# A gated linear attention feeding an MLP on one Trainium2 core: two token blocks worked one after the other, and a new hand-written order

## The chip, the cores and the metric

The kernel runs on one core of a Trainium2 chip. The core has five engines that run their own instruction streams: TensorE (PE in the profile: matrix products, with PEld for the loading of weights), VectorE (DVE), ScalarE (ACT), GpSimd (POOL) and the queue engine SyncE (SP), which here issues nearly all DMAs. They wait for one another through semaphores. The metric is device time in microseconds (us). The kernel before took 552.0 us, the median of three runs (550.45 to 552.59).

## The reference

First a gated linear attention for 4 batches, 8 heads, 768 time steps and head size 48, in float32:

```python
for t in range(S):
    state = alpha[:, :, t, :, None] * state + np.einsum('bhd,bhe->bhde', k[:, :, t], v[:, :, t])
    y[:, :, t] = np.einsum('bhd,bhde->bhe', q[:, :, t], state)
```

Its output, as 3072 tokens of 384 features, goes through a gated MLP with 1536 hidden features:

```python
g = x @ w_gate
silu = g * (1.0 / (1.0 + np.exp(-g)))
val = x @ w_val
return (silu * val @ w_out).astype(np.float32)
```

The three weight matrices come as 64-bit numbers. The kernel has to make 32-bit ones of them itself.

## The kernel before

**Attention.** The 768 steps of a batch are cut into four units of 192 steps, 16 units in all. For a unit u the kernel loads alpha, k and q (words La, Lk, Lq of the order) and v (V), turns them so that features lie on partitions, and runs two scans over alpha on DVE (G, the backward one, L429; f, the forward one, L436). k is multiplied with the one (mk), q with the other (q). Then come chunks of 64 steps: K (k turned back), S (scores), a mask (ma), the chunk states (ad, de), Y (outputs), and the split of Y into a high and a low part (yh on ACT, yl on DVE). The first four units (NPE = 4) are turned by TensorE (Ta, Tk, Tq, L378) from a buffer called wide that is filled by p words. Later units are turned by DVE (tr, tk, tq, L355, and kr for K, L498). In before the first four units also use their own forms of scores (L523), of the carry of the state (Bw, L599) and of the outputs (L693 to L710). Later units do scores and carry in one group (L551, L559) and outputs in another (L680), and add the chunk states on DVE where the early form copies them on ACT.

**MLP.** Tokens are worked in seven blocks (BLOCKS), the first two of 384 tokens, which are units 0 and 1, and 2 and 3. A step is one block and one slice f of 128 hidden features: g (gate product), v (value product), sl (SiLU on ACT), h (product on DVE), hh and hl (high and low part), o (output product). Each of g, v and o is nine matmuls of 384 or 512 columns, since every factor is split into a high and a low part and three of the four products are taken.

**Weights.** The 36 pieces of 128 x 384 weights are loaded and cut to 32 bits in 20 groups, w0 to w19: wl loads, v0, v1 and v2 are three integer steps that cut the 64-bit numbers down (L70 to L88), a makes the high part (L291) and p the low part (L295). After w2 a group holds two pieces. w16 is the gate and value slice 10, w17 the output slice 9 and the gate slice 11, w18 the value slice 11 and the output slice 10. A raw group lies in the place that the finished group behind it will have; that of w18 lies where wide is.

**Order.** The text ORDER lists every piece of work as engine:word (t TensorE, v DVE, s ACT, g POOL, y SP), and each engine takes its words strictly in that order. A digit behind @ names a PSUM bank. In before, HSEG = 7: blocks 0 and 1 first take slices 0 to 6 (steps 0 to 6 and 7 to 13), then 7 to 11 (steps 14 to 18 and 19 to 23). Between the halves the partial output sums go to DRAM (ot, os), are loaded back (pl) and added.

Of the kernel before, what the change touches and what calls it, by code (L numbers as in the profile page):

```python
# [8 lines left out]
F32 = mybir.dt.float32  # L9
# [18 lines left out]
NPE = 4  # L28

WIDE = [(u + x, i) for u in range(0, NPE, 2) for x, i in ((0, 0), (1, 0), (0, 2), (0, 1), (1, 1), (1, 2))]  # L30
# [4 lines left out]
FRAME = 2.0 ** 33  # L35
# [60 lines left out]
def main_path(ctx, tc, q, k, v, alpha, w_gate, w_val, w_out, out, flag, spill):  # L96
# [117 lines left out]
    HSEG = 7


    wsp = {}

    wlist = [("g", 0), ("v", 0)]
    for f in range(1, NF):  # L220
        wlist += [("g", f), ("v", f), ("o", f - 1)]
    wlist.append(("o", NF - 1))
    wgroups = [wlist[i : i + 1] for i in range(WSINGLE)] + [wlist[i : i + 2] for i in range(WSINGLE, len(wlist), 2)]

    def weight_dma(dst, kind, f):
        w = {"g": w_gate, "v": w_val, "o": w_out}[kind]
# [107 lines left out]
    state = {}

    def load_t(src, u, i):
        b, t0 = units[u]
        if u < NPE:

            L = Lt_early[i] if i < len(Lt_early) else Lt_early[4 + (i - 4) % 4]  # L340
            rows_load(L, src, u, halves=i == 0)
            return L
        L = Lt[(i + NPE // 2) % NL]
        Lv = L.rearrange("r (g x) -> r g x", g=G)
        if i < 3 * NPE + NL:
# [14 lines left out]
    def widened(u, i, L, eng):  # L360

        Wd = state[u]["wide", i] = Wide[:, WIDE.index((u, i)) % NP]
        n = 2 if u == i == 0 else 1
        for x in range(n):
            js = slice(x * J // n, (x + 1) * J // n)
            (eng.copy if eng is nc.scalar else eng.tensor_copy)(
                out=Wd[:, js, :, 0:D], in_=L.rearrange("p (e j c) -> p j e c", e=2, j=J)[:, js]
            )

    def pe_transposed(u, i, banks):  # L370

        Wd = state[u].pop(("wide", i))
        r = []
        for hf in range(2):
            js = slice(hf * J // 2, (hf + 1) * J // 2)
            pt = ps.tile([P, J // 2, P], F32, tag=banks[hf], name=f"pt{u}_{i}_{hf}")
            for j in range(js.start, js.stop):
                nc.tensor.transpose(pt[:, j - js.start, :], Wd.rearrange("p j e c -> p (j e c)")[:, j * P : (j + 1) * P], ident)  # L378
            r.append((js, pt.rearrange("p j (t g) -> p g t j", g=G)))
        return r  # L380
# [82 lines left out]
    def values_copied(u, eng):  # L463

        Vd = state[u]["V"]
        g0 = 0 if u >= NPE else GF
        for j, r in ((0, slice(BO, P)), (1, slice(0, BO))):
            (eng.copy if eng is nc.scalar else eng.tensor_copy)(
                out=U[j * BO : j * BO + C, :, g0 * D : G * D].rearrange("p c (g e) -> p c g e", e=D),
                in_=Vd[r, :, g0:, VC[j]],  # L470
            )
# [55 lines left out]
    def scores_carry(u, banks):  # L527

        st = state[u]
        KTt, X, Ks, Vd = st["Gs"], st["X"], st["K"], st["V"]  # L530
        st["S"] = [ps.tile([P, 512], F32, tag=banks[f], name=f"s{f}_{u}") for f in range(2)]
        st["sps"] = [t_[:, 0 : GF * T].rearrange("p (g t) -> p g t", g=GF) for t_ in st["S"]]
        A2 = ps.tile([P, 512], F32, tag=banks[2], name=f"A2_{u}")
        cps = [A2[:, x * G * D : (x + 1) * G * D].rearrange("p (g e) -> p g e", e=D) for x in range(2)]
        rest = A2[:, 2 * G * D : (2 * G + GF) * D].rearrange("p (g e) -> p g e", e=D)
        st["whole"] = False
        st["cps"] = [[(slice(0, G), cps[0])], [(slice(0, G), cps[1])], [(slice(GF, G), rest)]]
        if not last_of_batch(u):

            if u > NPE:  # L540
                beside = state[u - 1]["beside"]
            else:
                beside = ps.tile([P, GF * D], F32, tag=banks[3], name=f"A3_{u}").rearrange("p (g e) -> p g e", e=D)
            st["cps"][2].append((slice(0, GF), beside))
        for c in range(NU):
            cs = slice(1 + c * C, 1 + (c + 1) * C)
            cx = slice(c * C, (c + 1) * C)
            for g in range(G):
                for j in range(2):
                    r = slice(j * BO, j * BO + D)  # L550
# [12 lines left out]
    def carry(u, bank, whole=False):

        st = state[u]
        Ks, Vd = st["K"], st["V"]
        st["whole"] = whole
        A2 = ps.tile([P, 512], F32, tag=bank, name=f"A2_{u}")


        at = [512 - (c + 1) * G * D for c in range(NU)]
        cps = [A2[:, a : a + G * D].rearrange("p (g e) -> p g e", e=D) for a in at[:2]]
        last = A2[:, at[2] + GF * D : at[1]].rearrange("p (g e) -> p g e", e=D)
        beside = st["S"][0][:, GF * T : GF * (T + D)].rearrange("p (g e) -> p g e", g=GF)
        st["cps10"] = A2[:, at[1] :].rearrange("p (c g e) -> p c g e", c=2, g=G)
# [38 lines left out]
    def causal(u, i):  # L614

        X, sps = state[u]["X"], state[u]["sps"]
        r, z, f = (
            (slice(0, P), 1, 0) if u >= NPE else (slice(BO, P), 0, 0), (slice(0, BO), 1, 0), (slice(0, P), 1, 1)
        )[i]
        n = r.stop - r.start  # L620
        nc.vector.tensor_tensor(  # L621
            out=X[r, z, f * GF : (f + 1) * GF, :].rearrange("r g (c t) -> r g c t", c=NU),
            in0=sps[f][r].rearrange("r g (c t) -> r g c t", c=NU),
            in1=mask[r].unsqueeze(1).unsqueeze(1).to_broadcast([n, GF, NU, C]), op=ALU.mult,
        )
# [20 lines left out]
    def decay(u, eng):  # L646

        for j in range(2):
            r = slice(j * BO, j * BO + D)
            eng.scalar_tensor_tensor(  # L650
                out=state[u]["V"][r, 0, :, VC[j]], in0=SE[r], scalar=1.0 / FRAME,
                in1=state[u]["Gs"][r, :, 0:1].to_broadcast([D, G, D]), op0=ALU.mult, op1=ALU.mult,
            )
# [606 lines left out]
```

## Time and profile before

| | |
|---|---|
| median of three runs | 552.0 us (550.45 to 552.59) |
| span of the profiled execution | 549.9 us |
| TensorE busy | 531.2 us |
| DVE busy | 387.7 us |
| ACT busy | 264.1 us |
| POOL busy | 129.6 us |
| DMA | 77.66 MB, 141 GB/s on average |

Busy times are sums over the whole span. What a change is worth has to be read from the stretch in which it lies: which engine is waited for there, and how much idle time the others have.

### The profile page before, as it was taken

How to read it: one execution, taken by the hardware profiler on the slowest of the kernel's cores; microseconds unless marked ns; L12 is line 12 of the kernel's file. 1: busy time of each engine (PE TensorE's matmuls, PEld its weight loads, DVE VectorE, ACT ScalarE, POOL GpSimd, SP SyncE). 2: the span in 40 equal slices, each digit the busy share in tenths (PEclk: the TensorE clock that was granted, in tenths of full speed). 3: DMA queues.
4: the chain of work that ended last, by engine and by line, in shares of the span. 5: the costliest groups of instructions: out<-in, count | busy, mean ns of one | idle time of the engine just before them, and what ended most of it. 6: DMA issues, size and time to landing. Idle time of an engine off the chain costs nothing.

```text
span 549.9 us, 13452 instructions
## 1 busy us (share of the span) xinstructions
PE 531.2 (97%) x5365; PEld 477.5 (87%) x5365; DVE 387.7 (71%) x619; ACT 264.1 (48%) x568; POOL 129.6 (24%) x139
## 2 busy tenths in 40 slices
PE   5879999999999999999999999999999999999995
PEld 3769999999999999998888888888888888899994
DVE  6989899998898997987789856476968353212122
ACT  5778754245334335423423513343335475447691
POOL 5454344142440122110202321012100030011011
PEclk9989999999999999999999999999999999999999
DMA  8889557574455656535464543546246434355321
GB/s 228 245 232 261 159 149 230 132 217 139 125 147 148 162 141 169 174 97 127 139 162 118 129 125 67 135 116 157 54 113 152 99 99 110 95 155 126 103 65 49
DMA packets 115111, 77.66 MB, mean 141 GB/s; under 512 B 53728, under 2 KB 111968, under 8 KB 115040
## 3 DMA queue, kind: packets, MB, share of 16 engines
q1 hardware_dynamic: 114192, 75.98, 51.9%
q8 instruction: 44, 0.72, 0.6%
q10 hardware_dynamic: 848, 0.74, 0.4%
q14 instruction: 27, 0.22, 0.2%
HBM read 62.52 MB, written 5.90 MB: 124 GB/s over the span
## 4 chain that ended last, share of the span: by engine, by line
PE 94%; DVE 2%; ACT 1%; DMA 1%; POOL 0%; issue 0%; DVEq 0%; POOLq 0%; ACTq 0%
PE g L791 27%; PE v L791 27%; PE ops L847 14%; PE ops L842 14%; PE y L680 3%; PE s L551 2%; PE A L599 1%; PE A L559 1%; PE pt L378 1%; PE kps L482 1%; DVE Gs L429 1%; DMA Le<-in_alpha_dram 1%; PE s L523 0%; ACT AT L927 0%; DVE t L78 0%; PE y L710 0%
## 5 line engine op out<-in xcount | busy, mean ns | idle before, releaser
L791 PE MATMUL g<-xT,w 128*128 128x384 f32 (+1 forms) x756 | 163.4, 360 | 0.0
L791 PE MATMUL v<-xT,w 128*128 128x384 f32 (+1 forms) x756 | 162.8, 359 | 0.0
L791 PEld LDWEIGHTS v<-xT,w 128*128 128x128 f32 x756 | 136.1, 188 | 13.2
L791 PEld LDWEIGHTS g<-xT,w 128*128 128x128 f32 x756 | 135.9, 188 | 13.2
L803 DVE TENSOR_TENSOR h<-h,v 128x384 f32<-128x384 f32 (+1 forms) x84 | 51.2, 609 | 110.6 <-PE v L791 94.3
L814 POOL TENSOR_TENSOR hl<-h,hh 128x384 fp32r<-128x384 f32 (+1 forms) x44 | 50.4, 1146 | 267.0 <-ACT hh L808 250.1
L799 ACT ACTIVATE h<-g 128x384 f32<-128x384 f32 (+1 forms) x84 | 45.0, 536 | 137.7 <-PE g L791 119.7
L808 ACT CAST hh<-h 128x384 fp32r<-128x384 f32 (+1 forms) x84 | 46.6, 555 | 77.6 <-PE ops L842 35.3
L847 PE MATMUL ops<-w,hh 128*128 128x384 f32 x286 | 79.6, 337 | 0.0
L842 PE MATMUL ops<-hh,w 128*128 128x512 f32 x216 | 72.2, 393 | 0.0
L498 DVE STREAM_TRANSPOSE K<-Gs 32x384 f32<-32x384 f32 x96 | 54.7, 570 | 2.0
L847 PEld LDWEIGHTS ops<-w,hh 128*128 128x128 f32 x286 | 52.2, 188 | 0.4
L842 PEld LDWEIGHTS ops<-hh,w 128*128 128x128 f32 x216 | 40.5, 188 | 8.9
L847 PE MATMUL ops<-w,hl 128*128 128x384 f32 x143 | 47.8, 335 | 0.0
L842 PE MATMUL ops<-hl,w 128*128 128x512 f32 x108 | 42.2, 391 | 0.0
L295 POOL TENSOR_TENSOR w<-t,w 128x768 fp32r<-128x768 f32 (+1 forms) x16 | 30.5, 1907 | 34.5 <-ACT w L291 30.8
L814 DVE TENSOR_TENSOR hl<-h,hh 128x384 fp32r<-128x384 f32 (+1 forms) x40 | 26.8, 670 | 8.9 <-ACT hh L808 8.6
L429 DVE TENSOR_TENSOR_SCAN Gs<-AT,Z 128x776 f32<-128x776 f32 x16 | 28.3, 1770 | 4.2 <-ACT AT L927 4.1
L436 DVE TENSOR_TENSOR_SCAN AT<-AT,Z 128x774 f32<-128x774 f32 x16 | 29.9, 1868 | 0.6
L261 ACT ACTIVATE wc<-wc 128x384 f32<-128x384 f32 x36 | 19.9, 553 | 15.6 <-DMA wc<-in_moe_w_gate_dram 8.1
L847 PEld LDWEIGHTS ops<-w,hl 128*128 128x128 f32 x143 | 26.9, 188 | 0.0
L621 DVE TENSOR_TENSOR X<-s,mask 128x384 f32<-128x384 f32 (+1 forms) x36 | 19.3, 552 | 8.6 <-PE s L551 8.1
(140 smaller groups left out, 695.2 us busy)
## 6 DMA issues: line engine op xcount, KB each, us to landing
xT<-X SPq DMA_DIRECT2D x72, 72.0 KB, 2.2
raw<-in_moe_w_gate_dram SPq DMA_DIRECT2D x12, 384.0 KB, 5.0
raw<-in_moe_w_val_dram SPq DMA_DIRECT2D x12, 384.0 KB, 6.2
V<-in_v_dram SPq DMA_DIRECT2D x96, 48.0 KB, 3.3
raw<-in_moe_w_out_dram SPq DMA_DIRECT2D x12, 384.0 KB, 4.7
wc<-in_moe_w_gate_dram SPq DMA_DIRECT2D x12, 384.0 KB, 3.7
wc<-in_moe_w_out_dram SPq DMA_DIRECT2D x12, 384.0 KB, 3.6
wc<-in_moe_w_val_dram SPq DMA_DIRECT2D x12, 384.0 KB, 4.2
```

The source lines that it names most:

```text
L261: nc.scalar.activation(dev, dev, AF.Abs, accum_out=wviol[:, 1, i : i + 1])
L295: eng.tensor_tensor(out=lo, in0=src, in1=hi.bitcast(F32), op=ALU.subtract)
L429: nc.vector.tensor_tensor_scan(Gf[:, ::-1], Af[:, ::-1], Z[:, : 0 : -1], 0.0, op0=ALU.mult, op1=ALU.add)
L436: nc.vector.tensor_tensor_scan(Af, Af, Z[:, 1 : n + 1], Z[:, 0:1], op0=ALU.mult, op1=ALU.add)
L498: nc.vector.transpose(out=bass.AP(k0.tensor, k0.offset, [k0.ap[0], (G * 2 * D, NU), (2 * D, G), (1, 32)]), in_=Kg[j * BO + x : j * BO + x ...
L791: nc.tensor.matmul(pt, wsp[kind, f][a][:, kt * P : (kt + 1) * P], xT[blk][:, b_, kt, :], start=(n == 0), stop=(n == 3 * KT - 1),)
L799: nc.scalar.activation(h, acc.pop(("g", blk, f)), AF.Silu)
L803: nc.vector.tensor_tensor(out=h, in0=h, in1=acc.pop(("v", blk, f)), op=ALU.mult)
L808: nc.scalar.copy(out=hh, in_=acc["h", blk, f])
L814: eng.tensor_tensor(out=hl, in0=acc.pop(("h", blk, f)), in1=hh.bitcast(F32), op=ALU.subtract)
L842: nc.tensor.matmul(ops[blk][i], wsp["o", f][a][:, i * P : (i + 1) * P], h[b_], start=(first and n == 0), stop=(last and n == 2),)
L847: nc.tensor.matmul(ops[blk][i], h[b_][:, i * P : (i + 1) * P], wsp["o", f][a], start=(first and n == 0), stop=(last and n == 2),)
```

## The change

The change does four things. HSEG becomes 12, so that block 0 takes all 12 slices in steps 0 to 11 and block 1 in steps 12 to 23; the partial sums never go to DRAM. A new constant NST = 2 says which units use the early forms of scores, carry, outputs and copies: only units 0 and 1. Units 2 and 3 are still turned by TensorE, but are otherwise worked like later units. The buffers of wide are taken by when they were last read and not by a table, and the carry of the early units may use a bank of its own. ORDER is new up to about step 37; from there on it is the same on all engines.

```diff
-WIDE = [(u + x, i) for u in range(0, NPE, 2) for x, i in ((0, 0), (1, 0), (0, 2), (0, 1), (1, 1), (1, 2))]
+NST = 2
...
-g:im g:is y:La0 g:ik s:pa0 y:La1 t:Ta0@51 y:Lq0 g:iv y:wl2 s:ea0 s:pq0 t:Tq0@52 v:G0 ...
+g:ik y:La0 g:is g:iv y:wl0 s:pa0 v:w0v0 y:Lk0 v:w0v1 y:Lq0 t:Ta0@42 y:La1 v:w0v2 ...
...
-    HSEG = 7
+    HSEG = 12
...
+    wide_read = list(range(-NP, 0))
...
-        L = Lt[(i + NPE // 2) % NL]
+        L = Lt[i % NL]
...
-        Wd = state[u]["wide", i] = Wide[:, WIDE.index((u, i)) % NP]
+        w = min((x for x in range(NP) if wide_read[x] is not None), key=lambda x: wide_read[x])
+        wide_read[w] = None
+        Wd, state[u]["wide", i] = Wide[:, w], w
...
-        g0 = 0 if u >= NPE else GF
+        g0 = 0 if u >= NST else GF
...
-            if u > NPE:
+            if u > NST:
                 beside = state[u - 1]["beside"]
...
-    def carry(u, bank, whole=False):
+    def carry(u, bank, bank2, whole=False):
...
-        beside = st["S"][0][:, GF * T : GF * (T + D)].rearrange("p (g e) -> p g e", g=GF)
+        beside = None
+        if bank2 is not None:
+            beside = ps.tile([P, GF * D], F32, tag=bank2, name=f"A3_{u}").rearrange("p (g e) -> p g e", g=GF)
...
-        if u < NPE:
+        if u < NST:
             todo[f"qc{u}"] = lambda eng: q_odd(u, eng)
...
-            if i < 3 and (i != 1 or u < NPE):
+            if i < 3 and (i != 1 or u < NST):
                 todo[f"ma{u}.{i}"] = lambda eng, i=i: causal(u, i)
...
-        todo[f"S{u}"] = lambda eng, *banks: (scores if u < NPE else scores_carry)(u, banks)
-        if u < NPE:
-            todo[f"Bw{u}"] = lambda eng, bank: carry(u, bank, True)
-        todo[f"Y{u}"] = lambda eng, *banks: (outputs if u < NPE else outputs_quarters)(u, banks)
+        todo[f"S{u}"] = lambda eng, *banks: (scores if u < NST else scores_carry)(u, banks)
+        if u < NST:
+            todo[f"Bw{u}"] = lambda eng, bank, bank2=None: carry(u, bank, bank2, True)
+        todo[f"Y{u}"] = lambda eng, *banks: (outputs if u < NST else outputs_quarters)(u, banks)
```

What this does to the order of instructions is shown at three places. The first is the start of DVE's stream. Gs0 and Gs1 are the results of the backward scans of units 0 and 1, X0 is the product with q, t0 and t2 are weight groups 0 and 2 being cut. Before:

```order
L160 MEMSET Z_87 128x4
L429 SCALAR_TENSOR_TENSOR Gs0_158<-AT_94,Z_87 128x776
L433 RECIPROCAL Z_87<-Gs0_158 128x4
L436 SCALAR_TENSOR_TENSOR AT_94<-AT_94,Z_87 128x774
L453 TENSOR_TENSOR X0_104<-pt0_2_0_150,AT_94 112x128x3
L453 TENSOR_TENSOR X0_104<-pt0_2_1_154,AT_94 112x128x3
L78 SCALAR_TENSOR_TENSOR t2_163<-raw2_145,t2_163 128x384
L429 SCALAR_TENSOR_TENSOR Gs1_201<-AT_94,Z_87 128x776
```

The same place on DVE after the change:

```order
L159 MEMSET Z_87 128x4
L71 TENSOR_SCALAR t0_134<-raw0_130 128x384
L81 SCALAR_TENSOR_TENSOR t0_134<-raw0_130,t0_134 128x384
L87 SCALAR_TENSOR_TENSOR t0_134<-raw0_130,t0_134 128x384
L432 SCALAR_TENSOR_TENSOR Gs0_169<-AT_94,Z_87 128x776
L436 RECIPROCAL Z_87<-Gs0_169 128x4
L439 SCALAR_TENSOR_TENSOR AT_94<-AT_94,Z_87 128x774
L456 TENSOR_TENSOR X0_104<-pt0_2_0_161,AT_94 112x128x3
```

All three cutting steps of weight group 0 have moved ahead of the first scan.

The second place is DVE about the twelfth step of the MLP. h1_3 and h1_4 are hidden products of block 1, h0_8 and h0_9 of block 0 (the second number is the slice), t13 to t18 are weight groups being cut, w16 a finished one. Before:

```order
L78 SCALAR_TENSOR_TENSOR t13_1391<-raw13_1163,t13_1391 128x768
L440 MEMSET AT_94 128x3x2
L803 TENSOR_TENSOR h1_3_1448<-h1_3_1448,v1_3_1433 128x384
L88 SCALAR_TENSOR_TENSOR t14_1371<-raw14_1271,t14_1371 128x768
L814 TENSOR_TENSOR hl1_2_1468<-h1_2_1417,hh1_2_1466 128x384
L88 SCALAR_TENSOR_TENSOR t13_1391<-raw13_1163,t13_1391 128x768
L355 STREAM_TRANSPOSE AT_94<-L1_85 128x4x6x32
L498 STREAM_TRANSPOSE K0_106<-Gs4_1199 32x12x32 x2
L803 TENSOR_TENSOR h1_4_1500<-h1_4_1500,v1_4_1513 128x384
```

About as far along DVE's stream after the change:

```order
L810 TENSOR_TENSOR h0_8_1338<-h0_8_1338,v0_8_1307 128x384
L87 SCALAR_TENSOR_TENSOR t16_1336<-raw16_1090,t16_1336 128x768
L77 SCALAR_TENSOR_TENSOR t17_1365<-raw17_1259,t17_1365 128x768
L821 TENSOR_TENSOR hl0_7_1439<-h0_7_1276,hh0_7_1340 128x384
L77 SCALAR_TENSOR_TENSOR t18_1348<-raw18_703,t18_1348 128x768
L294 TENSOR_TENSOR w16_1437<-t16_1336,w16_1437 128x768
L87 SCALAR_TENSOR_TENSOR t17_1365<-raw17_1259,t17_1365 128x768
L810 TENSOR_TENSOR h0_9_1450<-h0_9_1450,v0_9_1427 128x384
```

At this depth before was cutting groups 13 to 15; now the groups 16 to 18 are there, and slice 8 or 9 of block 0 beside them.

The third place is SP's queue, with the semaphores that each DMA waits for (those called DMAHW only keep the places in the DMA rings apart). raw9 and raw18 are the loads of weight groups 9 and 18, L0 and L1 the rows of unit 4, V1 values of unit 3. Before:

```order
L398 DMA V1_90<-in_v_dram 64x4x48 [waits DMAHW6_49,PE_49,Pool_49]
L398 DMA V1_90<-in_v_dram 64x4x48 [waits DMAHW7_49,PE_49,Pool_49]
L233 DMA raw9_721<-in_moe_w_val_dram 128x3x256 [waits DMAHW0_49]
L230 DMA raw9_721<-in_moe_w_out_dram 128x768 [waits DMAHW1_49]
L398 DMA V1_90<-in_v_dram 64x4x48 [waits DMAHW2_49]
L398 DMA V1_90<-in_v_dram 64x4x48 [waits DMAHW3_49]
L398 DMA V1_90<-in_v_dram 64x4x48 [waits DMAHW4_49]
L398 DMA V1_90<-in_v_dram 64x4x48 [waits DMAHW5_49]
L349 DMA L1_85<-in_k_dram 32x4x288 [waits DMAHW6_49,Pool_49]
```

SP's queue after the change:

```order
L401 DMA V0_89<-in_v_dram 64x4x48 [waits DMAHW6_49]
L401 DMA V0_89<-in_v_dram 64x4x48 [waits DMAHW7_49]
L232 DMA raw18_703<-in_moe_w_val_dram 128x3x256 [waits PE_49,DMAHW0_49,Activation_49,Pool_49]
L229 DMA raw18_703<-in_moe_w_out_dram 128x768 [waits DMAHW1_49]
L349 DMA L0_84<-in_alpha_dram 32x4x288 [waits DMAHW2_49,Pool_49]
L349 DMA L0_84<-in_alpha_dram 32x4x288 [waits DMAHW3_49]
L351 DMA L0_84<-in_alpha_dram 32x4x256 [waits DMAHW4_49]
L351 DMA L0_84<-in_alpha_dram 32x4x256 [waits DMAHW5_49]
L232 DMA raw9_750<-in_moe_w_val_dram 128x3x256 [waits DMAHW6_49]
L229 DMA raw9_750<-in_moe_w_out_dram 128x768 [waits DMAHW7_49]
```

The load of group 18 has moved far forward, ahead of group 9 and of unit 4's rows. It waits for TensorE: the value that it waits for is reached with the last transpose of unit 3's q (Tq3), the last reader of wide, which TensorE has in its stream behind g0, v0, g1 and the scores of unit 2.

## Rows read from the trace of the kernel before

**Rows 1.** The page: header, and busy time of each engine

```profile
span 549.9 us, 13452 instructions
PE 531.2 (97%) x5365; PEld 477.5 (87%) x5365; DVE 387.7 (71%) x619; ACT 264.1 (48%) x568; POOL 129.6 (24%) x139
```

**Rows 2.** Stretches: length, busy PE, PEld, DVE, ACT, POOL; PEclk, DMA share, GB/s

```profile
6.80:40.00 33.20, 26.56 (x450) 22.52 (x451) 30.71 (x41) 23.93 (x57) 14.31 (x21) 0.95 0.89 246
40.00:107.20 67.20, 66.95 (x684) 64.93 (x683) 62.08 (x85) 40.13 (x81) 26.29 (x22) 1.00 0.67 189
28.00:42.00 14.00, 10.60 (x241) 9.17 (x240) 12.15 (x20) 10.29 (x26) 7.86 (x9) 0.88 0.83 237
42.00:56.00 14.00, 14.00 (x233) 13.34 (x222) 13.55 (x21) 11.89 (x29) 5.69 (x5) 1.00 0.98 262
```

**Rows 3.** Timeline of TensorE: start, duration, engine, line, operation, count

```profile
45.42 1.81 PE L791 MATMUL g<-xT,w 128*128 128x384 f32 x9
...
49.11 0.93 PE L523 MATMUL s<-X,Gs 48*64 48x64 f32 x48
...
50.47 0.38 PE L599 MATMUL A<-V,K 128*48 128x96 f32 x4
...
52.69 0.57 PE L482 MATMUL kps<-ident,Gs 112*64 112x112 f32 x4
...
103.27 1.72 PE L791 MATMUL g<-xT,w 128*128 128x384 f32 x9
104.83 1.72 PE L791 MATMUL v<-xT,w 128*128 128x384 f32 x9
...
111.17 0.27 PE L551 MATMUL s<-X,Gs 48*64 48x64 f32 x2
...
112.71 0.45 PE L847 MATMUL ops<-w,hh 128*128 128x384 f32 x1
```

**Rows 4.** Timeline of DVE, the idle time before in brackets

```profile
6.82 1.77 DVE L429 TENSOR_TENSOR_SCAN Gs<-AT,Z 128x776 f32<-128x776 f32 x1 [3.80 <-ACT AT L927]
...
11.72 0.55 DVE L78 SCALAR_TENSOR_TENSOR t<-raw,t 128x384 uint32<-128x384 uint32 x1
...
17.81 2.48 DVE L78 SCALAR_TENSOR_TENSOR t<-raw,t 128x384 uint32<-128x384 uint32 x2
...
38.99 1.02 DVE L728 TENSOR_TENSOR Y<-y,Y 112x384 fp32r<-112x384 f32 x2 [1.71 <-ACT Y L724]
...
106.67 0.55 DVE L803 TENSOR_TENSOR h<-h,v 128x384 f32<-128x384 f32 x1
```

**Rows 5.** DVE by line and shape: count, busy us, mean ns, idle before

```profile
L498 DVE STREAM_TRANSPOSE K<-Gs 32x384 f32<-32x384 f32 x96 | 54.7, 570 | 2.0
L436 DVE TENSOR_TENSOR_SCAN AT<-AT,Z 128x774 f32<-128x774 f32 x16 | 29.9, 1868 | 0.6
...
L803 DVE TENSOR_TENSOR h<-h,v 128x384 f32<-128x384 f32 x48 | 26.5, 552 | 50.4 <-PE v L791 39.8 <-ACT ac L422 4.0 <-ACT ac L423 3.7
...
L355 DVE STREAM_TRANSPOSE AT<-L 128x768 f32<-128x768 f32 x12 | 19.6, 1631 | 0.1
...
L88 DVE SCALAR_TENSOR_TENSOR t<-raw,t 128x768 uint32<-128x768 uint32 x16 | 15.2, 952 | 0.2
...
L644 DVE TENSOR_TENSOR V<-A,V 48x192 f32<-48x192 f32 x42 | 14.8, 351 | 3.9 <-PE A L559 3.2
...
L78 DVE SCALAR_TENSOR_TENSOR t<-raw,t 128x768 uint32<-128x768 uint32 x14 | 13.6, 979 | 0.1
...
L295 DVE TENSOR_TENSOR w<-t,w 128x768 fp32r<-128x768 f32 x4 | 4.6, 1153 | 0.0
```

**Rows 6.** Timeline of POOL, the idle time before in brackets

```profile
18.03 1.85 POOL L455 TENSOR_TENSOR X<-trq,AT 112x768 f32<-112x768 f32 x1 [1.77 <-DVE AT L436]
```

**Rows 7.** Timeline of SP's queue: start of issue, duration

```profile
3.17 0.60 SPq L233 DMA_DIRECT2D raw<-in_moe_w_gate_dram  x1
```

**Rows 8.** Timeline of ScalarE, the idle time before in brackets

```profile
8.65 0.56 ACT L70 ACTIVATE t<-raw 128x384 uint32<-128x384 uint32 x1 [0.77 <-DMA raw<-in_moe_w_gate_dram]
```

More of the change, by code (lines that the diff above doesn't have):

```diff
@@ L370, in pe_transposed @@
     def pe_transposed(u, i, banks):
-        Wd = state[u].pop(("wide", i))
-        r = []
+        w = state[u].pop(("wide", i))
+        Wd, r = Wide[:, w], []
         for hf in range(2):
@@ L379, in pe_transposed @@
             r.append((js, pt.rearrange("p j (t g) -> p g t j", g=G)))
+        wide_read[w] = max(-1, *(x for x in wide_read if x is not None), -1) + 1
         return r
@@ L617, in causal @@
         r, z, f = (
-            (slice(0, P), 1, 0) if u >= NPE else (slice(BO, P), 0, 0), (slice(0, BO), 1, 0), (slice(0, P), 1, 1)
+            (slice(0, P), 1, 0) if u >= NST else (slice(BO, P), 0, 0), (slice(0, BO), 1, 0), (slice(0, P), 1, 1)
         )[i]
@@ L650, in decay @@
             eng.scalar_tensor_tensor(
-                out=state[u]["V"][r, 0, :, VC[j]], in0=SE[r], scalar=1.0 / FRAME,
+                out=Vt[u % NV][r, 0, :, VC[j]], in0=SE[r], scalar=1.0 / FRAME,
                 in1=state[u]["Gs"][r, :, 0:1].to_broadcast([D, G, D]), op0=ALU.mult, op1=ALU.mult,
@@ L715, in rows_hi @@
     def rows_hi(u, i):
-        if i == 0:
-            st = state[u]
+        st = state[u]
+        if "Y" not in st:
             st["Y"] = st["X"] if u >= 2 else p2.tile(
@@ L728, in rows_lo, with swapped @@
         nc.vector.tensor_tensor(out=lo, in0=yps, in1=hi.bitcast(F32), op=ALU.subtract)
+    def swapped(u, g):
+        return g % 2 if u >= NST else g == G - 1
     def yrow(u, h):
-        return ((h + (h // 2 % 2 if u >= NPE else h // 2 == G - 1)) % 2) * BO
+        return ((h + swapped(u, h // 2)) % 2) * BO
     xT = {}
@@ L757, in pe_repack @@
             c0 = SEL + kt * P - 2 * D * g
-            nc.tensor.matmul(xp, sels[g == G - 1][:, c0 : c0 + P], Y[:, :, g, :], start=(n == 0), stop=(n == len(gs) - 1))
+            nc.tensor.matmul(xp, sels[swapped(u, g)][:, c0 : c0 + P], Y[:, :, g, :], start=(n == 0), stop=(n == len(gs) - 1))
     def x_copied(u, kt, copy):
```

2 lines of the change are left out of this document (1 added, 1 removed).

## Prediction

> **What bounds the kernel now.** I read the page's header first. TensorE is busy 531.2 of 549.9 us [rows 1], so at most 18.7 us are to be had unless its work shrinks. The profiled span of 549.9 stands beside a median of 552.0; I take the 2.1 us as what lies around the span and add them to every time below. Then the stretches: in 28 to 42 us TensorE works 10.6 of 14 us at a mean granted clock of 0.88, in 42 to 56 it works all 14.0 at 1.00 [rows 2]. The timeline of TensorE gives the boundary: the first gate product g0 starts at 45.42 [rows 3], and behind it a pass of nine matmuls follows the last every 104.83 - 103.27 = 1.56 us. So the kernel has two parts: a fill of 45.4 us, and 549.9 - 45.4 = 504.5 us in which TensorE sets the end. VectorE (DVE) is close behind it: between 40.0 and 107.2 us it is busy 62.08 of 67.2 us [rows 2]. The reader is to see that only these last 5.1 us keep TensorE from waiting for DVE.
>
> **The fill.** In before DVE starts the first scan at 6.82 and ends the last step of unit 1's rows (yl1.1) at 38.99 + 1.02 = 40.0 [rows 4]; g0 comes 5.4 us later, through transposes and copies. In that stretch DVE is busy 30.71 of 33.2 us [rows 2], so DVE sets it. The change takes these from DVE ahead of yl1.1: two steps of w0 (0.55 each, as the one at 11.72 [rows 4]), its cast (estimated 0.35), w4v0 (estimated 0.55), w3v1, w3v2, w4v2 (0.98, 0.95, 0.95 [rows 5]) and q2 (two of 0.55): 6.0 us. It puts in w5v1 and w5v2 (0.98 + 0.95), q1 and mk1, which POOL did (0.95 each, estimated from DVE's other steps on 768 columns), and mk2 (two of 0.55): 4.9 us. So 30.7 - 1.1 = 29.6 us of work.
> The start of it moves. w0's three steps now stand ahead of the first scan, and wait for a load. In before the first weight load was fourth in SP's queue, issued at 3.17 [rows 7], and ScalarE started on it at 8.65, at the end of a wait for it [rows 8]: 5.5 us. As second it is issued two places of 0.65 us earlier, at 1.9, with less ahead of it: it lands between 5.4 (below which nothing is late) and 7.4. I take 6.6; then about 1.4 us of steps, and the scan starts at 8.0 instead of 6.82 (bounds 6.8 and 8.8).
> Moving q1 and mk1 off POOL also saves collisions: two w steps of DVE took 2.48 us at 17.81 while POOL multiplied from 18.03 to 19.88 [rows 4, 6], against 0.55 for one alone: 1.4 lost. I take that 1.4 as saved (bounds 0 and 3). With 1.0 us of waiting (2.5 before), yl1.1 ends at 8.0 + 29.6 + 1.0 - 1.4 = 37.2 (bounds 35.3 and 39.5), and g0 can start some 5 us later, at 42.2: 3.2 us sooner.
> The Trainium skill (SBUF — State Buffer, section Who interferes with whom) says that a VectorE instruction with two SBUF inputs and a GpSimd instruction that reads SBUF exclude each other, and the second waits until the first has ended. The pair at 17.81 agrees: it ended when POOL did.
>
> **TensorE's work behind g0.** The separate carries go: unit 2's runs from 50.47 to 52.69 [rows 3], 2.2 us, unit 3's I estimate at half. Their matmuls return inside the scores: 111.17 to 112.71, 1.54 us, against 0.93 for scores alone, 0.6 each. Unit 2's scores move behind g0 (+0.9), and of single transposes slightly more go back than come forward (+0.6). Sum -0.6 (bounds -2 and 0): 503.9 us. The dropped spill and reload of partial sums cost TensorE nothing, since the matmuls are the same 27 a step; their copies, adds and stores lay beside it.
>
> **The weights.** Here the change asks for something before did not. Block 0 now takes all 12 slices of the weights in its first 12 steps; before, those steps were 7 slices for block 0 and 5 for block 1. In the new order g10 needs w16, whose low part DVE makes. I count DVE's list from yl1.1 to w16's low part against the list of before from yl1.1 to h11 (the twelfth step, 106.67 + 0.55 = 107.2 [rows 4]), for which the trace has 62.1 us of work. Only in before: 13 short steps of 0.56 [rows 5] (h, hl, masks, yl), two casts 1.1, mk2 1.1, w5v1, w5v2 and w15v0 2.5, two low parts 2.3, f4 2.0, tr5 1.6, six K transposes 3.4, in sum 21.3. Only in after: seven weight steps 6.8, seven low parts of 1.15, 8.1, q2 1.1, hl7 0.6, and the additions of units 2 and 3 that ScalarE did as copies, eight of 0.35 [rows 5] and four on half the columns, estimated 0.25, 3.8: 20.4. So w16 stands 62.1 - 0.9 = 61.2 us of DVE work behind yl1.1.
> TensorE's own way, if nothing held it, from g0 to g10 is 28 passes of 1.56, 43.7, four score or output groups of about 1.54, 6.2, and some 1.9 of transposes (estimate): 51.8 us. It could start g10 at 42.2 + 51.8 = 94.0. DVE gives it w16 at 37.2 + 61.2 + 1.0 = 99.4 (1.0 us of waiting taken; bounds 0, and the 5.1 of before). So TensorE waits 5.4 us in block 0, in pieces at g5, g6, g8 and g10, since the weights of each slice come from DVE just in time. From g10 on 503.9 - 51.8 = 452.1 us are left. Behind block 0 DVE has the weights done, and its list is lighter than before's. Span: 99.4 + 452.1 = 551.5, 1.6 over before; time 552.0 + 1.6 = 553.6.
> ScalarE has room (40.1 of 67.2 us [rows 2]). POOL makes seven low parts there, as many as lie in its 26.3 us of before.
>
> **Rivals.**
> Faster: DVE's waits vanish and its work is done with fewer collisions, so TensorE is not held. Then 42.2 + 503.9 = 546.1, time 548.2. For it: POOL's share of the fill's products goes, and DVE's 62.1 us hold collisions too. Against it: DVE has to give up over 5 us for that, more than I can find in the rows.
> Slower, by the loads: in the new order w18's load stands ahead of w9, w11, w10 and w12 in SP's queue and waits for the last use of the buffer it goes into, unit 3's q transposes, which TensorE does behind g1 and unit 2's scores, at about 42.2 + 3 x 1.56 + 1.54 + 0.7 = 49.1. All later loads wait with it. To w12 there are 4.4 MB behind it: at the 262 GB/s of 42 to 56 us [rows 2] 17 us, so w12 is there at about 66 to 68; DVE comes to it, by the same count up to w12's first step, at about 37.2 + 31 = 68. There is no slack: at 200 GB/s it takes 22 us, DVE and g10 are 5 us later, time 558.6. It decides when w12 lands after 68.
> Slower, by the lock: POOL's seven low parts each catch a DVE step, and hold it as at 17.81, 1.4 us a time; 7 x 1.4 is 9.8, of which about half is in the 62.1 already: 5 us more, time 558.6. The Trainium skill (SBUF — State Buffer, section Who interferes with whom) would make a loss of every such overlap; that the stretch of before still left DVE 5.1 us idle speaks for few of them.
> No gain in the fill: the wait for w0 and the later loads keep g0 at 45.4. Since DVE sets g10, the time would be about that of the two slower ones less 2, 556.
>
> **How the numbers follow.** About 0.5%, 2.8 us, is what can be told from no change: 549.2 to 554.8 is the same. My forecast, DVE setting block 0, has 0.57, with a range of its own of 550 to 557: 0.45 of it falls within 0.5%, 0.10 above, 0.02 below. The faster rival has 0.18, the loads 0.13, the lock 0.07, no gain in the fill 0.05. So faster 0.20, same 0.45, slower 0.35. The range reaches from the faster rival to the slower ones: 548.0 to 558.6.
>
> **What would show it.** The first scan at about 8 us behind w0's steps; yl1.1's end near 37 and g0 near 42; TensorE waiting before g5, g6, g8 or g10 for a low part of DVE, some 5 us in sum, and g10 near 99; DVE with hardly any idle time between 40 and 100; SP's queue waiting for unit 3's q transposes until about 49. Behind g12 no waits, and 452 us from g10 to the end. A waiting TensorE may also fall to the lower of its two clock levels (1.2 of 2.4 GHz), as the 0.88 of 28 to 42 us [rows 2], behind waits, shows; as long as DVE sets g10, that costs little. I am wrong if DVE has idle time in block 0 while TensorE runs through (faster), or if ScalarE's first cut of w9 or w12 waits for a load (slower).

## The result, and the profile after

The change made the kernel slower: 555.85 us (median of four runs, 553.75 to 556.24) against 551.81 for the kernel before on the same chip, a ratio of 1.0078 with a 95% interval of 1.0058 to 1.0099. The forecast was 553.6. Here and below medians are of all executions, while the ratios, which are estimated from the executions and not from the medians, leave out two slow ones, one of run 1 and one of run 7. The profiled execution has a span of 554.5 us; before had 549.9. The page's header and busy times, which answer [rows 1]:

```profile
span 554.5 us, 13501 instructions
PE 527.4 (95%) x5397; PEld 472.5 (85%) x5397; DVE 380.6 (69%) x613; ACT 263.7 (48%) x560; POOL 137.7 (25%) x147
```

TensorE works 3.8 us less than before and the kernel takes 4.6 us more, so it is waiting. Where begins with the fill: the timeline of DVE (start, duration, idle time before in brackets) at the first scan and at the end of yl1.1, and TensorE's first gate product, answering [rows 3, 4].

```profile
6.71 0.44 DVE L71 TENSOR_SCALAR t<-raw 128x384 uint32<-128x384 uint32 x1 [3.68 <-DMA raw<-in_moe_w_gate_dram]
...
8.25 1.77 DVE L432 TENSOR_TENSOR_SCAN Gs<-AT,Z 128x776 f32<-128x776 f32 x1
...
34.71 1.01 DVE L732 TENSOR_TENSOR Y<-y,Y 112x384 fp32r<-112x384 f32 x2
```
```profile
41.44 1.83 PE L798 MATMUL g<-xT,w 128*128 128x384 f32 x9
...
98.59 1.73 PE L798 MATMUL g<-xT,w 128*128 128x384 f32 x9
```

The scan starts at 8.25, yl1.1 ends at 35.7 and g0 starts at 41.44: the fill is 4.0 us shorter than in before. The row at 98.59 is g10. Behind g0 the gain is lost twice over. The stretch from g0 to the end (length, busy PE with its count, granted clock, DMA share, GB/s), first of before, then of the changed kernel:

```profile
45.42:549.90 504.48, 497.98 (x4832) 1.00 0.50 132
```
```profile
41.44:554.50 513.06, 499.63 (x4918) 1.00 0.49 128
```

It is 8.6 us longer: 1.65 us of it is more busy time, the rest is idle time. For 42 to 550 us the view of waits of the changed kernel (total, times, longest) names it; for the same stretch of before that view is empty.

```profile
PE v L798 <- DVE h L810: 3.0, 3, 1.8
PE ops L854 <- POOL hl L821: 1.7, 1, 1.7
PE g L798 <- ACT h L806: 1.3, 1, 1.3
PE s L554 <- ACT h L806: 1.1, 1, 1.1
```

These are five waits and a short one, 7.1 us in sum. TensorE's timeline puts them at v3, g5, S4 (the scores of unit 4), v22 and o28:

```profile
61.72 1.83 PE L798 MATMUL v<-xT,w 128*128 128x384 f32 x9 [1.84 <-DVE h L810]
...
69.98 1.32 PE L798 MATMUL g<-xT,w 128*128 128x384 f32 x6 [1.33 <-ACT h L806]
...
114.37 0.27 PE L554 MATMUL s<-X,Gs 48*64 48x64 f32 x2 [1.12 <-ACT h L806]
...
165.81 1.49 PE L798 MATMUL v<-xT,w 128*128 128x384 f32 x7 [0.85 <-DVE h L810]
...
212.46 0.44 PE L854 MATMUL ops<-w,hl 128*128 128x384 f32 x1 [1.68 <-POOL hl L821]
```

The engine named, or the one that it waited for, had itself stood still: for v3 DVE had waited for ScalarE's first cut of w9, and for o28 POOL for ScalarE's high part. ScalarE's timeline just before four of the five, and DVE's before v22:

```profile
59.15 0.89 ACT L69 ACTIVATE t<-raw 128x768 uint32<-128x768 uint32 x1 [3.45 <-DMA raw<-in_moe_w_out_dram]
...
66.81 0.91 ACT L69 ACTIVATE t<-raw 128x768 uint32<-128x768 uint32 x1 [1.72 <-DMA raw<-in_moe_w_out_dram]
...
111.82 0.57 ACT L260 ACTIVATE wc<-wc 128x384 f32<-128x384 f32 x1 [3.09 <-DMA wc<-in_moe_w_gate_dram]
...
206.93 0.55 ACT L260 ACTIVATE wc<-wc 128x384 f32<-128x384 f32 x1 [2.15 <-DMA wc<-in_moe_w_out_dram]
```
```profile
163.76 1.61 DVE L355 STREAM_TRANSPOSE trk<-L 128x768 f32<-128x768 f32 x1 [1.54 <-DMA L<-in_k_dram]
```

Every row ends in a DMA. At 59.15 it is the raw w9, at 66.81 w12, at 111.82 and 206.93 the weights that two range checks read (wc5 and wc28, which compare loaded weights with bounds and stand in ScalarE's stream among the SiLUs), at 163.76 the k rows of unit 7. The word that TensorE needs, or one that leads to it, stands behind each of them on an engine that takes its words in order. For w9 SP's queue shows why it is late:

```profile
39.37 1.80 SPq L401 DMA_DIRECT2D V<-in_v_dram  x2
48.90 0.38 SPq L232 DMA_DIRECT2D raw<-in_moe_w_val_dram  x1
49.32 0.68 SPq L229 DMA_DIRECT2D raw<-in_moe_w_out_dram  x1
50.10 0.85 SPq L349 DMA_DIRECT2D L<-in_alpha_dram  x2
51.00 0.90 SPq L351 DMA_DIRECT2D L<-in_alpha_dram  x2
51.95 0.43 SPq L232 DMA_DIRECT2D raw<-in_moe_w_val_dram  x1
```

The rows at 48.90 and 49.32 are w18: SP stands from 41.2 to 48.9 us for the last transpose of unit 3's q, and w9, at 51.95, stands behind it. That is the mechanism of the rival on the loads. The stretches, answering [rows 2], show the same from the side of the DMA engines: 164 GB/s in 42 to 56 us, where before had 262, and 317 in the next 14, in which TensorE works 10.76 of 14 us.

```profile
42.00:56.00 14.00, 13.64 (x245) 12.77 (x247) 13.77 (x26) 12.10 (x24) 6.00 (x5) 1.00 0.60 164
56.00:70.00 14.00, 10.76 (x88) 9.91 (x77) 12.88 (x15) 8.17 (x16) 5.76 (x5) 1.00 1.08 317
```

For wc5 it is the ten transfers of unit 3's outputs ahead of its load, which take SP until 107.4:

```profile
100.83 6.56 SPq L782 DMA_DIRECT2D xT<-X  x10
107.49 0.54 SPq L232 DMA_DIRECT2D wc<-in_moe_w_gate_dram  x1
```

### The profile page after: what moved, and what is told of

It is laid out like the page before. It is cut to its first block, busy times and chain, and to the rows that moved or that the text cites. A ratio compares the mean times of both kernels' runs of the same rounds, so it can differ in the third digit from the quotient of the medians.

```text
span 554.5 us, 13501 instructions
## 1 busy us (share of the span) xinstructions
PE 527.4 (95%) x5397; PEld 472.5 (85%) x5397; DVE 380.6 (69%) x613; ACT 263.7 (48%) x560; POOL 137.7 (25%) x147
## 4 chain that ended last, share of the span: by engine, by line
PE 74%; DMA 9%; SPq 6%; DVE 4%; issue 3%; ACT 2%; POOL 1%; DVEq 0%; ACTq 0%
PE g L798 22%; PE v L798 22%; PE ops L849 14%; PE ops L854 9%; DMA raw<-in_moe_w_out_dram 5%; SPq L782 3%; PE y L685 2%; PE s L554 2%; PE A L562 1%; SPq L401 1%; DMA raw<-in_moe_w_gate_dram 1%; DMA wc<-in_moe_w_gate_dram 1%; PE pt L380 1%; DMA V<-in_v_dram 1%; DVE Gs L432 1%
## 5 line engine op out<-in xcount | busy, mean ns | idle before, releaser
L821 POOL TENSOR_TENSOR hl<-h,hh 128x384 fp32r<-128x384 f32 (+1 forms) x54 | 64.0, 1187 | 285.4 <-ACT hh L815 231.7
L821 DVE TENSOR_TENSOR hl<-h,hh 128x512 fp32r<-128x512 f32 (+1 forms) x30 | 20.6, 688 | 8.7 <-ACT hh L815 8.5
L294 POOL TENSOR_TENSOR w<-t,w 128x768 fp32r<-128x768 f32 (+1 forms) x11 | 20.7, 1879 | 21.7 <-ACT w L290 21.4
L554 PEld LDWEIGHTS s<-X,Gs 48*64 48x64 f32 x672 | 20.8, 134 | 5.4 <-issue 4.1
```

The source lines that it names most:

```text
L294: eng.tensor_tensor(out=lo, in0=src, in1=hi.bitcast(F32), op=ALU.subtract)
L554: nc.tensor.matmul(st["sps"][g // GF][j * BO : j * BO + C, g % GF, cx], KTt[r, g, cs], X[r, 0, g, cx], start=True, stop=True,)
L821: eng.tensor_tensor(out=hl, in0=acc.pop(("h", blk, f)), in1=hh.bitcast(F32), op=ALU.subtract)
```

## The experiments

Times are medians, and ratios are to the kernel before on the same chip.

**1. w18's load later.**

```diff
-... y:V2.1 ... y:wl18 ... y:La4 y:wl9 y:V3 y:wl11 y:wl10 y:wl12 ... y:wl14 y:V4.2 ...
+... y:V2.1 ... y:La4 y:wl9 y:V3 y:wl11 y:wl10 y:wl12 ... y:wl14 y:wl18 y:V4.2 ...
```

> One word is moved: the load of weight group 18 goes from ahead of unit 4's rows and w9 in SP's queue to behind the load of w14, so that w9, w11, w10 and w12 no longer stand behind its wait for unit 3's q transposes (SP idle from 41.2 to 48.9 us in the changed kernel, 855.85 - 300 = 555.85 us median). Theory A, the loads: TensorE's waits at v3 (1.84 us) and g5 (1.33 us) are the late loads of w9 and of w10 or w12; SP issues w9 near 41.5, ScalarE's waits of 3.45 and 1.72 us for them are gone, both TensorE waits go with the 0.16 us that each restart costs: 3.5 us, g10 at 95.1 instead of 98.6, time 552.3. Theory B, DVE's work (the prediction's): DVE makes w16's low part at 98.7 with only 1.4 us of waiting for ScalarE's cuts, so g10 can come no more than 1.4 us sooner, the waits turn up again at g6 to g10 with DVE busy all through; time 554.4. Theory C, the rate: the loads from 56 to 70 us fill the DMA engines anyway, so an earlier issue brings nothing; ScalarE waits as long, time 555.5 to 556.

(The subtraction in it is a slip; 555.85 is meant.) Measured: 555.48 us, ratio 1.0076 (1.0053 to 1.0099), no change against the changed kernel. From g0 to g10 TensorE took 56.97 us instead of 57.15. The wait at g5 is gone, the one at v3 stays (1.58), and in place of g5's come 0.23 at g4 and 0.32 at v5 and their restarts. Two things hold it. SP's queue has a new wait, unit 4's rows for a buffer that POOL clears:

```profile
37.21 1.93 SPq L401 DMA_DIRECT2D V<-in_v_dram  x2
45.41 0.81 SPq L349 DMA_DIRECT2D L<-in_alpha_dram  x2
46.26 1.80 SPq L351 DMA_DIRECT2D L<-in_alpha_dram  x2
48.11 0.43 SPq L232 DMA_DIRECT2D raw<-in_moe_w_val_dram  x1
```

And DVE is busy 56.18 of the 56.97 us. g0 was at 39.22 in this profile, 2.2 us sooner than in the changed kernel's, though its fill is the same; run 7 takes that up.

**2 and 3. The words in front, alone and with w18.** The second moves three words, the third adds the move of the first.

```diff
-... s:wc5 ... s:sl12 ... s:ad4.0 ... v:tk7 s:sl21 v:h21 ... s:wc10 ... s:hh26 ...
+... s:sl12 ... s:ad4.0 s:wc5 ... s:sl21 v:h21 v:tk7 ... s:hh26 s:wc10 ...
```

> Three words are moved, each behind the MLP word that it holds up: on ScalarE the range checks wc5 (behind ad4.0, it stood ahead of the SiLU of step 12) and wc10 (behind hh26), on DVE the transposes tk7 (behind h21). In the changed kernel ScalarE waits 3.09 us at 111.8 and 2.15 us at 206.9 for the loads of these checks and DVE 1.54 us at 163.8 for unit 7's k rows, and TensorE waits 1.12 us at S4, 1.68 us in an output pass at 210 and 0.85 us at v22. Theory A: these late loads, in front of MLP words on engines that work strictly in order, are the waits; 3.65 us and about 0.5 us for three restarts go: time 551.7. Theory B: the words behind are late for another reason (DVE behind), so the waits come back at the next step; time 555 to 556.

> The moves of the two runs before together. Theory A (all of TensorE's waits behind the first gate product are late loads): 3.5 + 4.1 us less than 555.85, 548.2 us, which is 0.7% under the kernel before; TensorE has under 1 us of waits between g0 and the end. Theory B (DVE sets block 0, the later waits are loads): 1.4 + 4.1 us less, 550.3.

Measured: 560.57 (ratio 1.0173, 1.0141 to 1.0205) and 560.5 us (1.018, 1.0157 to 1.0203), both slower than before and than the changed kernel's first 1.0078. S4's and v22's waits went as expected (run 3 still has o28's, 1.70). But wc10 was the wrong word: the check that waits at 206.9 is wc28. Moved, wc10 kept its buffer longer, and the next check's load waits for that buffer in SP's queue (of the second run):

```profile
183.65 4.77 SPq L401 DMA_DIRECT2D V<-in_v_dram  x4
193.78 0.40 SPq L232 DMA_DIRECT2D wc<-in_moe_w_val_dram  x1
194.28 6.66 SPq L782 DMA_DIRECT2D xT<-X  x10
200.99 1.07 SPq L349 DMA_DIRECT2D L<-in_alpha_dram  x2
```

SP stood from 188.4 to 193.8, and unit 6's outputs and unit 9's rows went late with it; TensorE then waited 1.18 us at g29 and 2.05 at Y7 (0.87 at S6 comes from tk7's move, as run 5 shows again). Neither theory had this: a word moved back on ScalarE moved a load back on SP.

**4. q1 and mk1 on POOL again.**

```diff
-... v:mk1 ... v:q1 ...
+... g:mk1 ... g:q1 ...
```

> In the fill the products q1 and mk1 go back from DVE to POOL, as before the change; nothing else is changed against the changed kernel (555.85 us, yl1.1 ends at 35.7, g0 at 41.44). By the prediction's terms DVE has 1.9 us less work and loses 1.4 us (0 to 3) to POOL's reads: yl1.1 ends at 35.2, g0 at 41.0, time 555.4. If collisions cost nothing, yl1.1 ends at 33.8 and g0 at 39.5, time 553.9, unless w5 and the later loads hold block 0 (then g0 is sooner and the time is the same). If they cost 3 us, yl1.1 ends at 36.8, g0 at 42.5, time 557.

Measured: 557.67 us (1.0117, 1.0085 to 1.015); yl1.1 ended at 37.1 us, 1.4 later than in the changed kernel's profile and up to 2.8 later than in the runs above, and g0 started at 40.88. With 1.9 us less for DVE to do it was later, so POOL's share cost it 3.3 to 4.6 us, over the upper bound of 3: a scan of DVE took 3.04 us beside POOL's product (1.83 in the changed kernel), and DVE waited 0.94 and 1.80 us for copies that POOL now did later.

```profile
16.74 3.04 DVE L439 TENSOR_TENSOR_SCAN AT<-AT,Z 128x774 f32<-128x774 f32 x1
```
```profile
16.31 1.84 POOL L963 TENSOR_TENSOR Gs<-trk,Gs 128x768 f32<-128x768 f32 x1 [5.56 <-ACT K L489]
```

The expectation by the prediction's 1.4 us was wrong in sign. This is one profile; the time itself is not told apart from the changed kernel's in run 7 (1.0109).

**5. The three right words.**

```diff
-... s:wc5 ... s:sl12 ... s:ad4.0 ... v:tk7 s:sl21 v:h21 ... s:wc28 ... s:hh29 ... s:hh28 ...
+... s:sl12 ... s:ad4.0 s:wc5 ... s:sl21 v:h21 v:tk7 ... s:hh29 ... s:hh28 s:wc28 ...
```

> The run with three words moved had one of them wrong: the check whose load ScalarE waits for at 206.9 us of the changed kernel is wc28, not wc10; wc10, moved behind hh26, held up the next check's load, the ten stores and loads of unit 6's outputs and unit 9's rows behind it in SP's queue (SP stood from 188.3 to 193.4). Here wc5 goes behind ad4.0, tk7 behind h21 and wc28 behind hh28, and wc10 stays. Theory A (each wait behind g12 is a late load ahead of an MLP word on an engine that works in order): the waits at S4 (1.12 us), v22 (0.85) and o28 (1.68) go with 0.5 us for restarts; time 555.85 - 4.1 = 551.7, and from g12 to the end 445.3 - 4.1 = 441.2 us. Theory B: TensorE comes earlier to later loads, and half or more of it returns as new waits up to step 40; from g12 to the end 443 us or more.

Measured: 552.35 us (1.0036, 1.0017 to 1.0054), span 549.7: some 0.4% given back. Its waits from g0 to the end:

```profile
PE v L798 <- DVE h L810: 2.3, 1, 2.3
PE A L562 <- issue: 0.9, 1, 0.9
```

The three waits behind g12 are gone; from g12 to the end it is 442.0 instead of 444.9 us, with a new wait of 0.87 at S6 (unit 6's last K transposes now stand behind tk7). Theory A holds.

**6. A candidate with more moves.**

```diff
-... s:wc0 ... s:hh37 ... v:q3 ... v:h2 ... s:kc3.0 ... s:sl4 ... v:mk4 ... v:tq4 ... v:w17p ...
+... s:hh37 s:wc0 ... v:h2 v:q3 ... s:sl4 s:kc3.0 ... v:w17p v:mk4 v:tq4 ...
```

> A candidate: the run before, with w18's load behind w14's, the check wc0 behind hh37, the hidden product h2 ahead of q3 on DVE (it stood behind w9v1), the SiLU of step 4 ahead of unit 3's K copies and w11v0 on ScalarE, and mk4 and tq4 (2.6 us of DVE) behind w16p and w17p. If DVE's work up to w16's low part sets block 0, g10 comes 2.6 us sooner against g0: g10 - g0 at 54.4 instead of 57.15 us, and the time is 551.7 - 2.6 = 549.1, unless S4 waits for unit 4's products, which come 2.6 us later (then 550.5). If the late loads alone set block 0, g10 - g0 is 53.6, time 548.2. If mk4 and tq4 only move DVE's lateness to g11 and S4, it is 551.7.

Measured: 559.44 us (1.0161, 1.0135 to 1.0187). The moves paid elsewhere: K3.0 waited 2.35 us for the copies of K3.2, which stand on ScalarE behind w9's high part (as in runs 10 and 11), and tq4, the reader of a row buffer, held unit 5's k rows in SP's queue, and behind them w19 and unit 3's outputs, so that g12 waited 1.74 and 1.14 us.

**7. The changed kernel again.**

Nothing is edited.

> The changed kernel again, word for word, for a second profile and a time beside the candidates. In seven profiled runs with the same fill (the runs with w18's load, the checks or DVE's steps altered) g0 started at 39.1 to 39.9 us, in the changed kernel's own profile at 41.44. If that profile is the exception, g0 is at 39 to 40 here, and since the time was no better in those runs, what is won there is lost behind g0: g0 to the end about 515 us, with the waits at v3, g5, S4, v22 and o28 in place; ratio to before 1.0076 to 1.008. If the fill differs by a word in the order after all, g0 is at 41.4 again.

Measured: 558.41 us (1.0109, 1.0063 to 1.0155), span 553.2, g0 at 38.65, the same five waits. In eleven profiles of this fill after the first, g0 was at 38.65 to 39.91, so 41.44 was the exception and the fill's gain is mostly 5.5 to 6.8 us against the one profile of before, whose own spread is not known. In the first profile SP was 8.03 us over four loads of v from 18.96 on (5.4 to 7.5 in the eleven) and issued the next rows at 27.04 (24.3 to 26.0), and ScalarE's first cut of w3, ahead of the last copies for g0, began at 38.10 (35.3 to 36.6). What held SP there was not found. Behind g0 this execution took 514.6 us against 513.1.

**8 and 9. Less work for DVE, without and with w18's move.**

```diff
-            t[1 + i](eng)
+            if i != 1 or n not in (7, 8, 10, 11, 12, 13, 14, 15, 16): t[1 + i](eng)
```

> The second of the three cutting steps is left out for the weight groups 7, 8 and 10 to 16, so these weights are not the reference's: 9 x 0.95 = 8.6 us less work on DVE between yl1.1 and w16's low part, and no load or wait is changed. If DVE's work alone sets block 0: no waits of TensorE from g4 to g10, g10 - g0 falls from 57.15 to about 54. If the late loads alone set it: the waits at v3 (1.84 us, behind w9's load) and g5 (1.33 us, behind w10's or w12's) stay, g10 - g0 at 56.5 to 57. Time 555.85 less the same difference.

> The same steps left out (groups 7, 8 and 10 to 16, so these weights are not the reference's), and w18's load behind w14's. With that load moved alone, g10 - g0 was 56.97 us, and DVE busy 56.18 of these. If DVE's work and the late loads each hold TensorE about equally long in block 0, only taking both away frees it: g10 - g0 at 53.4 to 53.8, with no wait over 0.4 us, and in the run without the load's move the waits at v3 and g5 stay. If DVE alone: 53.5 to 54 in both. If something else holds it (PSUM banks, ScalarE): 56 or more in both.

Measured: 555.48 (1.0084, 1.0053 to 1.0116) and 552.37 us (1.0031, 1.0008 to 1.0054). The stretch from g0 to g10 of the one, then of the other (length, busy PE, PEld, DVE, ACT, POOL; clock):

```profile
39.41:96.13 56.72, 54.53 (x641) 52.79 (x639) 50.12 (x68) 39.51 (x69) 21.74 (x17) 0.97 0.77 216
```
```profile
39.91:93.71 53.80, 53.04 (x642) 51.21 (x639) 50.03 (x68) 39.61 (x69) 23.04 (x17) 1.00 0.81 226
```

With nine steps of 0.95 us left out DVE was busy 4.8 us less in this stretch (54.92 in the changed kernel), not 8.6, since its other work took longer (low parts 1.16 us each over the span instead of 0.97). With this work gone but w9 late, v3 waits 2.19 us (w9's load: ScalarE waits up to 3.7 us for it), the rest of block 0 runs through, and 1.6 us are lost at a lower clock behind that wait. With both taken away the stretch is 53.8, in the range named, though g5 still waits 0.76 us where none over 0.4 was expected. So of the four combinations 57.15, 56.97, 56.72 and 53.80: neither cause alone is worth half a microsecond, the two together 3.35. Each is one profile, and the four profiles whose block 0 has neither edit (the changed kernel twice, runs 2 and 5) have 56.62 to 57.54; only the 53.80 lies outside that spread. (Without the fall of the clock, which not every such wait brings, DVE's work alone would be worth about 2.)

**10 to 12. Three candidates.** The first has the load's move of run 1, wc5 and wc28 as in run 5, wc0 as in run 6, and DVE's h2 and tk7 in other places; the second adds the first edit below that names mk4, the third the last.

```diff
-... v:q3 ... v:h2 ... v:G7 ... v:tk7 ... v:h21 v:yl5.1 v:f7 ... v:h22 v:kr6.1 ... v:kr6.0 ...
+... v:h2 v:q3 ... v:G7 ... v:kr6.1 v:h21 v:kr6.0 v:yl5.1 v:tk7 v:f7 ... v:h22 ...
...
-... v:mk4 ... v:tq4 ... v:w17p ... y:Lk5 v:h10 ... y:xr3 ... v:kr4.2 ... v:h11 v:f4 ... v:kr4.0 ...
+... v:w17p v:mk4 v:tq4 ... v:h10 v:f4 ... y:xr3 y:Lk5 ... v:h11 v:kr4.2 v:kr4.0 ...
...
-... s:w7a ... s:w9a s:kc3.2 ... v:f7 ... v:h22 ...
+... s:kc3.2 s:w7a ... s:w9a ... v:h22 v:f7 ...
```

> The run with three words moved (wc5, tk7, wc28), and with w18's load behind w14's, the check wc0 behind hh37, h2 ahead of q3 on DVE, and unit 6's last two K transposes ahead of tk7 (behind tk7 they were late for S6, which TensorE waited 1.1 us for). If late loads and words in the wrong place are all, the 2.3 us at v3 and the 1.1 at S6 go: 3.4 us less than 552.35, 549.0. If DVE's work up to w16's low part sets block 0 once the loads are in time, the waits at v3 come back at g4 to g10 (g10 - g0 56 to 57 us) and only S6's 1.1 us are won: 551.2.

> The run before, and 2.6 us of DVE's work taken from ahead of w16's low part: mk4 and tq4 behind w17p, with f4 right behind h10 so that unit 4's q product is not late for S4, and unit 5's k rows behind unit 3's outputs in SP's queue, so that no load waits for tq4. If DVE sets block 0: g10 - g0 comes down by 2.0 to 2.6 us against the run before, time 2 us less (549.2), unless S4 has to wait for unit 4's products (up to 2 us, then no gain). If the late loads were all, g10 - g0 is the same in both, 53.5 to 54.5.

> The run before (the second candidate with mk4 and tq4 moved) with its two own waits taken away: on ScalarE the copies of K3.2 go ahead of w7a and w9a (they stood behind w9a, which waits for DVE's last cut of w9 until 61.2 us, and TensorE waited 1.96 us at K3.0 for them), on DVE h22 goes ahead of f7 (a scan that took 3.3 us beside POOL's product, and TensorE waited 1.62 us at v23). If each was only a word behind the wrong neighbour, g10 - g0 falls from 56.8 to 54.3 and the time by 2.5 + 1.8 us: 550.3, level with the kernel before. If DVE's work still sets block 0, about half of the 2.5 us comes back at g5 to g10: 551.5. If the waits only move on again, 553.5 or more.

Measured: 554.38 (1.0068, 1.0044 to 1.0092), 554.58 (1.0073, 1.0049 to 1.0097) and 552.38 us (1.0036, 1.0018 to 1.0053); g10 - g0 57.59, 56.83 and 57.57 us. The times hoped for, 549.0, 549.2 and 550.3, were missed by 2.1 to 5.4 us. In the first two v3's wait is gone and a wait of 1.96 us at K3.0 is there, for the copies of K3.2 behind w9's high part on ScalarE; in the third that one is gone, and the SiLU of step 3, which stands behind w9's high part too, holds g4 for 2.31 us. In all three, and in run 6, ScalarE waits there for DVE's last step of w9, which took 2.48 to 2.65 us (1.18 in the changed kernel) beside a low part that POOL made. In the first POOL's ran from 57.95 to 60.54:

```profile
58.86 2.49 DVE L87 SCALAR_TENSOR_TENSOR t<-raw,t 128x768 uint32<-128x768 uint32 x1
```
```profile
62.94 0.57 PE L485 MATMUL kps<-ident,Gs 112*64 112x112 f32 x4 [1.96 <-ACT K L490]
```

Reordering gave back nothing in block 0. The 2.6 us taken from DVE in the second brought 0.8, less than the 1.6 that the first lost at g4 and v4 to a fall of the clock. No version that does all the work beats the kernel before; the best two (runs 5 and 12) stand at 1.0036.

## Why the prediction was right or wrong

The time lies in the stated range, 2.3 us above the forecast. By the prediction's own limit of 0.5% it is slower, which had a chance of 0.35, against 0.45 for no change.

**The fill** was right in its mechanism and too small in size: 3.2 us forecast, 4.0 in the first profile, 6.8 in the second, with w0's steps ahead of the scan (8.25, forecast 8.0) and yl1.1 at 35.7 (37.2). The term that was too small is the 1.4 us for collisions with POOL: run 4 puts POOL's share at 3.3 to 4.6. Not all of the gain need be the new order's: in before's one profile the granted clock was 0.88 on average in 28 to 42 us [rows 2], behind a wait of TensorE of 2.1 us, and 1.00 in all thirteen profiles after the change. What that is worth was not taken apart.

**Block 0** came out as forecast in its length: g10 at 98.59 (99.4), 57.15 us behind g0 (57.2). Two terms inside it were off and cancelled, which is luck: TensorE's own way, counted as 51.8, was 53.55 us of busy time, and its waits, counted as 5.4, were 3.5. DVE ended w16's low part at 98.72, no earlier than g10 wanted it, with 54.92 of the 57.15 us busy. The two largest waits there, though, were not those for low parts at g5 to g10 but v3 and g5, through late loads; that rival was given the deciding point that w12 lands after 68, and ScalarE started on w12 at 66.81 after waiting for it. Runs 1, 8 and 9 show that either cause alone keeps the stretch long, so each hides the other; how long DVE's work alone would keep it is clouded by the fall of the clock in run 8. The lock rival did not decide in the changed kernel: DVE was busy 59.5 us in the 63.0 from yl1.1 to w16's low part, under the 61.2 of work forecast. Once the loads were in time it did show, at w9 (runs 6 and 10 to 12).

**The step that failed** is "Behind g12 no waits", and with it the 452.1 us from g10 to the end; 455.9 were measured. 3.65 us are the waits at S4, v22 and o28, and run 5 took them away by moving three words, with 453.0 left. The prediction looked only for engines short of time behind block 0; here ScalarE and DVE had time, but stood in order behind a load. ScalarE waited for the checks' loads in before too, 15.6 us in sum, and TensorE never waited for it there: what counts is which word stands behind the check, and how soon TensorE needs it.

**TensorE's work** was forecast 0.6 us smaller and is 1.65 larger. The carry did go into the scores as counted; of the 2.25 us between, about 1 is what follows a wait, since the pass in which one falls takes 0.15 to 0.4 us beyond the wait itself. The rest lies ahead of g10: the 51.8 us took 1.56 for each of 28 passes, and a pass behind transposes or a group of scores took up to 1.69 (o5 started at 82.67, g7 at 84.36). From g10 on run 5, less its wait at S6, needs 452.1 us, as forecast.

**The faster rival**, 546.1 us of span, is what the parts add up to without their waits: g0 at 39.3, 53.8 to g10, then 453.0 less the 0.9 at S6. That is 545.2, worked out from run 5 and from run 9, which leaves out work that the kernel needs; no single run reached it.

## What to carry to other kernels

On engines that work in order a load is late for everything behind the instruction that waits for it: look in each stream for DMA-fed instructions (range checks, cuts, row transposes) and ask when their load is issued, not only whether the engine has room. Before moving such an instruction back, see which load waits for its buffer, and what stands behind that load in the queue. Where removing one cause changes nothing, remove two at a time before calling either harmless.

## What the runs showed of the hardware

TensorE's clock fell behind waits, but not behind each one. In the thirteen profiles after the change, 12 of the 21 waits of 1.62 to 2.98 us behind g0 were followed by some 3 us at the lower of the two levels (0.50, 1.2 GHz), and none of the 11 of 1.12 to 1.58 us that began at the full clock. The same wait at o28 in the changed kernel's first profile (1.68 us) and in its second (1.81 us), as stretches of busy PE and granted clock:

```profile
209.00:211.00 2.00, 1.78 (x97) 1.00 0.94 236
211.00:213.00 2.00, 0.54 (x3) 1.00 1.01 241
213.00:215.00 2.00, 2.00 (x14) 1.00 0.62 150
```
```profile
209.00:211.00 2.00, 1.12 (x6) 1.00 0.94 245
211.00:213.00 2.00, 2.00 (x9) 0.54 0.33 73
213.00:215.00 2.00, 2.00 (x9) 0.60 0.00 0
```

The second lost 1.6 us more at the two passes behind it (9 matmuls in 2 us instead of 14). A wait can so cost nearly twice its length, which fits the changed kernel's wide spread (551.9 to 558.8 us in run 7, where before had 549.5 to 553.4); the timed executions have no trace, so that this is the reason was not shown.

DVE and POOL still collided: in the second candidate (run 11) DVE's f7 took 3.34 us beside a product of POOL, against 1.83 at 10.27 in the changed kernel and a mean of 1.87 in before [rows 5].

```profile
164.42 3.34 DVE L439 TENSOR_TENSOR_SCAN AT<-AT,Z 128x774 f32<-128x774 f32 x1
```
```profile
164.44 1.70 POOL L963 TENSOR_TENSOR Gs<-trk,Gs 128x768 f32<-128x768 f32 x1 [7.03 <-DVE Z L436]
```

The excess of 1.5 us is about POOL's 1.70; the pair that the Trainium skill (SBUF — State Buffer, section Who interferes with whom) calls exclusive agrees with it. The pair at 17.81 in before, which the prediction lets end together, did not quite: DVE's second step ended at 20.29, 0.4 us behind POOL's product [rows 4, 6], about as a step of 0.55 us held until POOL was done would.
